# Three tile pairs instead of two, and keys' sums with the values stationary: one change to an attention and gated-MLP kernel on one Trainium2 core

## The chip, the cores and the metric

The kernel runs on one core of one Trainium2 chip. The core has a matrix engine (PE, in the code `nc.tensor`, TensorE) with its own queue for loading the stationary operand (PEld), a vector engine (DVE, `nc.vector`, VectorE), an activation engine (ACT, `nc.scalar`, ScalarE), a third elementwise engine (POOL, `nc.gpsimd`, GpSimd) and a queue that issues transfers (SP, `nc.sync`, SyncE). The metric is the device time of one execution in microseconds; lower is better. Each engine works through its own queue in order. The order in a queue is not quite that of the Python code: a planner (Tile) lists the instructions as they become ready, gives buffers out, and sets the semaphores.

## What is computed

Two things, one after the other: an attention with positive random features for 8 batches, 8 heads, 576 positions and 64 dimensions (128 features), and a gated MLP over its 4608 rows (512 to 1536 and back to 512). Cut to what matters:

```python
def phi(x):                                     # x is q or k, scaled
    h = einsum('bhsd,md->bhsm', x, omega) - sum(x * x, -1) / 2
    return exp(h - max(h, -1)) / sqrt(m)
q_p, k_p = phi(q), phi(k)
kv  = einsum('bhsm,bhsd->bhmd', k_p, v)         # keys' sums
z   = sum(k_p, axis=2)                          # (b, h, m)
num = einsum('bhsm,bhmd->bhsd', q_p, kv)
den = einsum('bhsm,bhm->bhs', q_p, z)[..., None] + 1e-06
x   = (num / den) as 4608 rows of 512
out = (silu(x @ w_gate) * (x @ w_val)) @ w_out
```

The three weights come as 64-bit floats.

## The kernel before

**Attention.** A head pair and 256 positions make a group (`kgroups`, `qgroups`, lines 115 to 117); each batch has nine groups of keys and nine of queries, the ninth (`None`) holding the left-over 64 positions of all four head pairs. `steps` (lines 124 to 127) puts two groups into each of 72 steps: keys alone in the first six, then a query and a key group, queries alone in the last six. A step n loads its rows (`load`, `load_v`), transposes them on PE (`st_transpose`, L400), copies them to x (ACT, L408), projects them (`st_project`, L423, two matmul instructions for each fp32 product), takes the maximum on DVE (`st_max`, L437 to L447) and the exponential on ACT (`st_exp`, L459, eight activations a step). `k_accumulate` (L561) takes the keys' features `ph` as the stationary operand and the values `vt`, 64 columns and a column of ones, as the moving one; so the 65th column of the sum is z. When a batch's half is whole, `kv_finalize` copies it out of PSUM.

**Two ways to divide.** For batches 0 to 3 (`b < BPOOL`) `q_mult` multiplies queries by kv and z at once and DVE divides. For batches 4 to 7 the queries' features are divided beforehand: `kv_finalize` transposes the z column (L481), ACT copies it (L483), SP writes it to DRAM (`zd`) and `load_z` reads it back to all 128 partitions (`zt`); `q_den` multiplies by it on POOL (L521, L517), reduces on DVE, and `q_norm` scales `ph` (L537). `q_out` (L642) then forms the output columns with kv stationary, 64 columns wide, one head in each half of PE's columns.

**MLP.** The 4608 rows are nine tiles of 512 columns. Each fp32 factor is split in a high and a low part (ACT casts, POOL or DVE subtracts), and each product is three matmul instructions of 512 columns. A *direct* tile is visited once for each of four sets of three of the twelve feature blocks (`stream`): 36 instructions for the gate, 36 for the value (`mm1`, L678), 36 for the way down (`mm2`, L687) of the previous visit. `ROUNDS` lists the direct tiles. `PAIRS` lists pairs of tiles for which gate and value go by seven half-size products (Strassen) instead of eight (`pair_rounds`, `product`, L912); the way down is as for direct tiles. Both have to load and split weights: before each new set, `load_weights` fetches a block from DRAM and at once emits the cast and the subtraction (`split_piece`, L251, L252).

**Pacing.** Attention and direct tiles are interleaved by hand. Up to step `EARLY` (25) a step holds attention only (`CLOSE`); afterwards each step goes through `GROUPED`, with six `SHARE` places at which `give` lets the MLP stream run on. How much is due is `course`: a taut line from step `EARLY` to the end of attention (step 76) through what is available, ending `MARGIN` = 45 us before the work of the direct tiles. `clock` and `marks` spread the conversion of the 36 weight blocks from 64 bits (`convert_all`, six ticks each: ACT L277 and L289, DVE L280 to L286, POOL L291) along the same line. When attention is over its buffers are given back, `first_x` prepares the first pair, and the pairs follow.

**Queues at the start.** `load_v` issues the first step's values, and the left-over values of a step below `AHEAD` (6), from ACT's queue; all other loads from SP's. In the first six steps there is one such left-over group, in step 2: four issues (L365). `setup_omega` (L337) and the copies of x follow in ACT's queue.

Of the kernel before, what the change touches and what calls it, by code (L numbers as in the profile page):

```python
# [11 lines left out]
F32 = mybir.dt.float32  # L12
# [4 lines left out]
ALU = mybir.AluOpType  # L17
# [6 lines left out]
def kernel(  # L24
# [37 lines left out]
    ROUNDS = [range(0, 3), range(3, 5)]  # L62
    PAIRS = [(5, 6), (7, 8)]
# [32 lines left out]
    make_identity(nc, ident)  # L96

# [211 lines left out]

    def load_weights(f, i):  # L310
        need(f, i)
        fetched = fetch((f,), i)
        new_weights(f, i)
        split_piece(f, i, fetched[0])
# [78 lines left out]
    def st_transpose(n):  # L393
# [11 lines left out]
        st = att.tile([P, 4, 2, CH, 2], F32, name=f"st_{n}", tag="st", bufs=6)  # L405
# [66 lines left out]
    def kv_finalize(b, a2):  # L472
        acc = kvacc.pop((b, a2))
        raw = att.tile([P, 4, VW], F32, name=f"kvr{b}_{a2}", tag="kvr", bufs=4)
        nc.scalar.copy(raw, acc)
        for j in range(2):
            kvst[b, 2 * a2 + j] = raw[:, 2 * j : 2 * j + 2, :]
        if b >= BPOOL:

            zp = ps_att(f"zp{b}_{a2}", [4, P])  # L480
            nc.tensor.transpose(zp, raw[:, :, D], ident)  # L481
# [6 lines left out]
    zds = {}  # L488
    zbc = {}

    def load_z(n):

        for _, b, g, gr in slots(n, "q"):
            if g == 0 and b >= BPOOL:
                zt = att.tile([P, 2, 4, M], F32, name=f"zt{b}", tag="zt")
                for a2 in range(2):
                    nc.sync.dma_start(
                        zt[:, a2], zds.pop((b, a2)).rearrange("(o h) m -> o h m", o=1).broadcast_to([P, 4, M])
                    )
                    zbc[b, a2] = zt[:, a2]  # L500
# [42 lines left out]
    def k_accumulate(n, half):  # L543

        n -= KLAG
        ks = [(b, g, gr, c) for _, b, g, gr in slots(n, "k") for c in range(CH)]
# [24 lines left out]
        return bool(slots(n, "k"))  # L571
# [133 lines left out]
    def down(j, k_, ht, wts, next_set, tt):  # L705
        fs = sorted(ht)
        po = ps_moe(f"o{j}_{k_}_{tt}", [P, DM])
        for n, f in enumerate(fs):
            need(f, 2)
            mm2(po, ht[f], weights[f, 2] if wts is None else wts[f], tt, n == 0, n == len(fs) - 1)  # L710
# [14 lines left out]
    def stream():  # L725

        todo = []
        for vi, (j, s_, k_) in enumerate(visits):
# [15 lines left out]
            for f in fs:  # L744
                need(f, 0)
                pg[f] = ps_moe(f"g{vi}_{f}", [P, T])[:, 0:w]
                mm1(pg[f], weights[f, 0], xs)
                yield mm1_us(w)
# [16 lines left out]
            for f in fs:  # L765
                need(f, 1)
                pv = ps_moe(f"v{vi}_{f}", [P, T])[:, 0:w]
# [11 lines left out]
            if final:  # L779
                make_seven((0, 0), 1, fetch((0, 1), 1))  # L780
            wts = {f: weights[f, 2] for f in fs} if vi else None
# [269 lines left out]
    def give(us):  # L1051
        debt[0] += us
        while debt[0] > 0:
            u = next(ma, None)
            if u is None:
                debt[0] = 0.0
                return False
            debt[0] -= u
# [50 lines left out]
    for n in range(NN):  # L1109
# [17 lines left out]
        load_z(n)  # L1127
# [41 lines left out]
```

## Time and profile before

| what | value |
|---|---|
| runs | 1180.82, 1174.82, 1174.39 us; median 1174.82 |
| the profiled execution: its time, its span | 1172.79 us, 1171.0 us |
| busy: PE, DVE, ACT, POOL | 98%, 54%, 58%, 49% of the span |
| first PE projection (start of step 0) | 8.83 us |
| steps 0 to 24, attention alone | 8.83 to 116.28 us |
| steps 25 to 71, with the direct tiles | from 116.28 us; step 71 begins at 703.48 us |
| pairs | from 797.31 us |

The table's stretches were read off the timeline: a step begins with the first of its 16 matmuls of L423, and the pairs with the first matmul of L912. In all views times are microseconds from the start of the span, "mean ns of one" is nanoseconds, and `x` in front of a number counts instructions. A matmul's busy time in the profile is longer than its share of the engine, because neighbours overlap; what a matmul costs is read from start to start.

### The profile page before, as it was taken

The page shows a single profiled execution, that of the slowest core. Times are in us where ns is not written, and L with a number is a line of the kernel's source. Part 1 is how long each engine was busy: PE and PEld are TensorE (multiplying, and loading weights), DVE is VectorE, ACT ScalarE, POOL GpSimd, SP SyncE. Part 2 cuts the span into 40 slices and gives each one's busy share as a digit, 9 for nine tenths or more (in the row PEclk, how much of TensorE's full clock was granted, in tenths as well). Part 3 has the DMA queues.
Part 4 walks back from the last instruction along what each step waited for, and adds up shares of the span by engine and source line. Part 5 has one row for each costly group of instructions (what it writes and reads, how often), then busy time and mean ns, then how long its engine had stood idle before and what let it go on. Part 6 is the DMA issues. An engine that isn't in the chain of part 4 may idle for free.

```text
span 1171.0 us, 18724 instructions
## 1 busy us (share of the span) xinstructions
PE 1149.5 (98%) x6705; PEld 951.7 (81%) x6705; DVE 630.0 (54%) x1159; ACT 678.3 (58%) x1499; POOL 569.1 (49%) x500
## 2 busy tenths in 40 slices
PE   7999999999999999999999999999999999999998
PEld 6998778888888888888888777878778888888886
DVE  5876667535466554334332552462566666456654
ACT  5898887775666665665466665334544445444441
POOL 3342353433365465554445765244655543455551
PEclk9999999999999999999999999999999999999999
DMA  7654355643454442443232212424311112211103
GB/s 168 155 147 116 108 168 164 177 127 111 127 155 131 125 118 70 120 105 82 64 80 73 60 46 81 127 81 123 93 53 47 48 53 54 72 55 54 45 19 73
DMA packets 174109, 113.52 MB, mean 97 GB/s; under 512 B 125856, under 2 KB 144320, under 8 KB 174016
## 3 DMA queue, kind: packets, MB, share of 16 engines
q1 hardware_dynamic: 172096, 111.86, 35.2%
q8 instruction: 53, 0.87, 0.3%
q10 hardware_dynamic: 1920, 0.46, 0.2%
q14 instruction: 40, 0.33, 0.1%
HBM read 87.10 MB, written 25.18 MB: 96 GB/s over the span
## 4 chain that ended last, share of the span: by engine, by line
PE 73%; DVE 5%; ACT 3%; DMA 2%; issue 2%; POOL 1%; SPq 1%; POOLq 0%; DVEq 0%; ACTq 0%
PE o L687 22%; PE g L678 11%; PE a L912 10%; PE v L678 10%; PE c L912 5%; PE pp L423 3%; PE d L912 3%; PE kvacc L561 2%; PE ptq L585 2%; PE xt L642 2%; PE pt L400 1%; DMA wraw<-wscr 1%; ACT ph L459 1%; DMA first_b<-xs 1%; POOL wlo L252 1%
## 5 line engine op out<-in xcount | busy, mean ns | idle before, releaser
L407 POOL TENSOR_TENSOR sq<-nat 128x512 f32<-128x512 f32 x72 | 75.9, 1055 | 199.3 <-DVE st L437 157.3
L716 DVE TENSOR_TENSOR acc<-o,acc 128x512 f32<-128x512 f32 x140 | 95.6, 687 | 128.6 <-PE o L687 128.2
L459 ACT ACTIVATE ph<-pp,st 128x128 f32<-128x128 f32 x576 | 157.0, 387 | 6.4 <-DVE st L447 5.7
L444 DVE TENSOR_REDUCE st<-pp 128x4 f32<-128x512 f32 x144 | 93.3, 686 | 95.7 <-PE pp L423 95.4
L252 POOL TENSOR_TENSOR wlo<-wraw,whi 128x512 fp32r<-128x512 f32 x76 | 103.1, 1366 | 64.0 <-ACT whi L251 62.4
L678 PE MATMUL g<-xh,whi 128*128 128x512 f32 x240 | 96.3, 401 | 0.9 <-DVE sl L771 0.9
L678 PE MATMUL v<-xh,whi 128*128 128x512 f32 x240 | 95.6, 398 | 0.5 <-DVE acc L716 0.5
L687 PE MATMUL o<-whi,hh 128*128 128x512 f32 x240 | 95.9, 400 | 0.0
L423 PE MATMUL pp<-omT,x 64*128 64x128 f32 x1152 | 90.9, 289 | 4.6 <-ACT x L408 4.6
L687 PE MATMUL o<-whi,hl 128*128 128x512 f32 x240 | 93.8, 391 | 0.9 <-POOL hl L775 0.9
L775 POOL TENSOR_TENSOR hl<-sl,hh 128x512 fp32r<-128x512 f32 x60 | 77.9, 1302 | 33.7 <-ACT hh L774 33.5
L678 PE MATMUL g<-xl,whi 128*128 128x512 f32 x240 | 94.0, 392 | 0.0
L678 PE MATMUL g<-xh,wlo 128*128 128x512 f32 x240 | 94.0, 392 | 0.0
L678 PE MATMUL v<-xh,wlo 128*128 128x512 f32 x240 | 93.9, 391 | 0.0
L687 PE MATMUL o<-wlo,hh 128*128 128x512 f32 x240 | 93.9, 391 | 0.0
L678 PE MATMUL v<-xl,whi 128*128 128x512 f32 x240 | 93.6, 390 | 0.0
L423 PEld LDWEIGHTS pp<-omT,x 64*128 64x128 f32 x1152 | 73.9, 189 | 21.8 <-issue 11.6
L899 POOL TENSOR_TENSOR wlo<-wspare,whi 128x512 fp32r<-128x512 f32 (+1 forms) x40 | 40.5, 1032 | 75.0 <-ACT whi L898 68.6
L771 DVE TENSOR_TENSOR sl<-v,sl 128x512 f32<-128x512 f32 x60 | 40.9, 685 | 60.8 <-PE v L678 60.8
L251 ACT CAST whi<-wraw 128x512 fp32r<-128x512 f32 x76 | 46.6, 629 | 42.1 <-PE v L678 24.4
L525 DVE TENSOR_REDUCE dj<-jk 128x4 f32<-128x512 f32 x36 | 24.6, 685 | 83.8 <-POOL jk L521 69.1
L774 ACT CAST hh<-sl 128x512 fp32r<-128x512 f32 x60 | 37.5, 626 | 51.9 <-DVE sl L771 51.7
(257 smaller groups left out, 2938.4 us busy)
## 6 DMA issues: line engine op xcount, KB each, us to landing
wraw<-wscr SPq DMA_DIRECT2D x80, 256.0 KB, 2.7
wspare<-wscr SPq DMA_DIRECT2D x40, 256.0 KB, 2.7
wscr<-wc SPq DMA_DIRECT2D x36, 256.0 KB, 2.2
out_dram<-acc SPq DMA_DIRECT2D x72, 128.0 KB, 2.3
nat<-in_k_dram SPq DMA_DIRECT2D x64, 128.0 KB, 3.1
nat<-in_q_dram SPq DMA_DIRECT2D x64, 128.0 KB, 3.1
v<-in_v_dram SPq DMA_DIRECT2D x62, 128.0 KB, 3.0
st<-in_moe_w_gate_dram SPq DMA_DIRECT2D x12, 512.0 KB, 3.9
```

Source lines behind the costliest of these rows:

```text
L251: nc.scalar.copy(hi, raw)
L252: nc.gpsimd.tensor_tensor(lo, raw, hi.bitcast(F32), op=ALU.subtract)
L407: nc.gpsimd.tensor_tensor(sq, nat, nat, op=ALU.mult)
L423: nc.tensor.matmul(pp[hh][:, i, c, :], x[r, i, c * P : (c + 1) * P], omT[r], start=True, stop=True)
L444: nc.vector.tensor_reduce(st[:, 1, :, :, hh], pp[hh], axis=AX.X, op=ALU.max, negate=True)
L459: step_end["s"] = nc.scalar.activation(ph[:, c, hh * M : (hh + 1) * M], pp[hh][:, i, c, :], AF.Exp, bias=st[:, 3, i, c, hh : hh + 1], scal ...
L678: nc.tensor.matmul(ps, a_[:, ws], b_[:, c, :], start=n == 0, stop=n == 3 * NC - 1)
L687: nc.tensor.matmul(ps, a_[:, ts_], b_, start=first and n == 0, stop=last and n == 2)
L716: nc.vector.tensor_tensor(a_, po, a_, op=ALU.add)
L771: nc.vector.tensor_tensor(h, pv, h, op=ALU.mult)
L775: nc.gpsimd.tensor_tensor(hl, h, hh.bitcast(F32), op=ALU.subtract)
L912: nc.tensor.matmul(ps, a_[:, w_], b_[:, c, :], start=start and c == 0 and m == 0, stop=c == CH - 1 and m == 2, skip_group_check=True,)
```

## The change

It has five parts.

1. **Rounds and pairs.** Tiles 3 and 4 leave the direct rounds and become a third pair, the first one.
2. **Keys' sums, batches 4 to 7.** `k_columns` takes the values as the stationary operand (64 columns; the two heads of a pair in the two halves of PE's columns) and the features as the moving one (128 columns). The sum is then transposed; `kv_turn` copies it out to `x`-tagged SBUF and transposes it back with four PE transposes a batch.
3. **z, batches 4 to 7.** `z_sum` adds up the features on DVE into two tiles a batch; `z_spread` multiplies each by a matrix of ones (fp32, 512 columns), which sums over the partitions and spreads the result over all of them; ACT copies it to `zt`. The transposes, the DRAM round trip and `load_z` are gone.
4. **Weights.** `load_weights` only issues the fetch; `land`, called at each unit of the stream, emits cast and subtraction three units later, or earlier when the weights are needed.
5. **Left-over values** by SP, also in the first steps; and `st` has three buffers instead of six.

```diff
-    ROUNDS = [range(0, 3), range(3, 5)]
-    PAIRS = [(5, 6), (7, 8)]
+    ROUNDS = [range(0, 3)]
+    PAIRS = [(3, 4), (5, 6), (7, 8)]
...
+    ones = const.tile([P, P], F32, name="ones")
+    nc.vector.memset(ones, 1.0)
...
     def load_weights(f, i):
         need(f, i)
-        fetched = fetch((f,), i)
-        new_weights(f, i)
-        split_piece(f, i, fetched[0])
+        landing.append([LAND, f, i, fetch((f,), i)[0]])
+
+    def land(upto=None):
+
+        for t in landing:
+            t[0] -= upto is None
+        while landing and (landing[0][0] <= 0 or upto in [(f, i) for _, f, i, _ in landing]):
+            _, f, i, raw = landing.pop(0)
+            new_weights(f, i)
+            with behind_step():
+                split_piece(f, i, raw)
...
-            load_group(t, v, b, gr, True, nc.scalar if n == 0 or n < AHEAD and gr is None else nc.sync)
+            load_group(t, v, b, gr, True, nc.scalar if n == 0 else nc.sync)
...
-        st = att.tile([P, 4, 2, CH, 2], F32, name=f"st_{n}", tag="st", bufs=6)
+        st = att.tile([P, 4, 2, CH, 2], F32, name=f"st_{n}", tag="st", bufs=3)
...
-        if b >= BPOOL:
-
-            zp = ps_att(f"zp{b}_{a2}", [4, P])
-            nc.tensor.transpose(zp, raw[:, :, D], ident)
-            zs = att.tile([4, P], F32, name=f"zs{b}_{a2}", tag="zs")
-            nc.scalar.copy(zs, zp)
-            zd = dram.tile([4, P], F32, name=f"zd{b}_{a2}", tag="zd", bufs=4)
-            nc.sync.dma_start(zd, zs)
-            zds[b, a2] = zd
...
+    def z_sum(n):
+
+        for _, b, g, gr in slots(n - 1, "k"):
+            if b < BPOOL:
+                continue
+            ph = box["k", b, g]
...
+            with behind_step():
...
+                pr, r = gr
+                to = zsums[b, pr // 2][:, pr % 2]
+                if pr < 2 and r == 0:
+                    nc.vector.tensor_tensor(to, ph[:, 0], ph[:, 1], op=ALU.add)
+                else:
+                    for c in range(CH):
+                        nc.vector.tensor_tensor(to, ph[:, c], to, op=ALU.add)
+
+    def z_spread(n):
+
+        for b, a2 in list(zsums):
+            if n != (qstep[b, 2] + JLAG if a2 else qstep[b, 0]):
+                continue
+            zp = ps_att(f"zp{b}_{a2}", [P, 4, M])
+            nc.tensor.matmul(
+                zp.rearrange("p h m -> p (h m)"), ones, zsums.pop((b, a2)).rearrange("p j m -> p (j m)"),
+                start=True, stop=True,
+            )
+            zbc[b, a2] = att.tile([P, 4, M], F32, name=f"zt{b}_{a2}", tag="zt", bufs=3)
+            nc.scalar.copy(zbc[b, a2], zp)
+
+    def k_columns(n):
+
+        for _, b, g, gr in slots(n - KLAG, "k"):
...
+            for c in range(CH):
+                for j, pr in enumerate(pairs_of(gr)[c]):
+                    for hh in range(2):
+                        nc.tensor.matmul(
+                            acc[hh * D : (hh + 1) * D, pr, :],
+                            vt[:, 2 * c + j if gr is None else c, hh, 0:D],
+                            ph[:, c, hh * M : (hh + 1) * M],
...
+            if done[b] == 2 * NACC:
+                turned[b] = att.tile([P, NPAIR, M], F32, name=f"kvt{b}", tag="x")
+                nc.scalar.copy(turned[b], kvacc.pop(b))
+
+    def kv_turn(n):
+
+        b, o = divmod(n - (AHEAD - 1), NG)
+        if o or b not in turned:
+            return
+        kt = turned.pop(b)
+        pt = ps_att(f"kvp{b}", [P, 2, 4, D])
+        for pr in range(NPAIR):
+            nc.tensor.transpose(
+                pt[:, pr // 2, 2 * (pr % 2) : 2 * (pr % 2) + 2].rearrange("p h d -> p (h d)"), kt[:, pr], ident
+            )
+        for a2 in range(2):
+            raw = att.tile([P, 4, VW], F32, name=f"kvr{b}_{a2}", tag="kvr", bufs=4)
+            nc.scalar.copy(raw[:, :, 0:D], pt[:, a2])
...
     GROUPED = (
         q_out,
+        k_columns,
         st_project,
         q_transpose,
         lambda n: k_accumulate(n, 0),
         lambda n: k_accumulate(n, 1),
+        kv_turn,
+        z_spread,
         st_max,
+        z_sum,
         st_exp,
         q_den,
...
-        load_z(n)
```

`land((f, i))` also stands behind each `need(f, i)` in `stream` and `down`, and once for the blocks of the way down ahead of each later visit; `give` calls `land()` for each unit. `k_accumulate` skips batches 4 to 7.

More of the change, by code (lines that the diff above doesn't have):

```diff
@@ new lines @@
+    zsums = {}
+    qstep = {(b, g): n for n in range(NS) for _, b, g, _ in slots(n, "q")}
+    turned = {}
+    def z_sum(n):
[3 more added lines that the diff above has]
+            ph = box["k", b, g]
+            if gr is None or gr == (0, 0):
+                a2 = 0 if gr else 1
+                zsums[b, a2] = att.tile([P, 2, 2 * M], F32, name=f"zs{b}_{a2}", tag="zs")
+                if a2:
+                    nc.gpsimd.memset(zsums[b, a2], 0.0)
+            with behind_step():
+                if gr is None:
+                    for c in range(CH):
+                        for j in range(2):
+                            rows = slice(j * RES, (j + 1) * RES)
+                            to = zsums[b, c][rows, j]
+                            nc.vector.tensor_tensor(to, ph[rows, c], to, op=ALU.add)
+                    continue
[6 more added lines that the diff above has]
+                        nc.vector.tensor_tensor(to, ph[:, c], to, op=ALU.add)
@@ new lines, in k_columns @@
+    def k_columns(n):
+        for _, b, g, gr in slots(n - KLAG, "k"):
+            if b < BPOOL:
+                continue
+            ph, vt = box.pop(("k", b, g)), vrows[b, g]
+            busy.remove(vt)
+            if b not in kvacc:
+                kvacc[b] = ps_k.tile([P, NPAIR, M], F32, name=f"kvt{b}", tag="kv")
+                done[b] = 0
+            acc = kvacc[b]
+            for c in range(CH):
+                for j, pr in enumerate(pairs_of(gr)[c]):
[4 more added lines that the diff above has]
+                            ph[:, c, hh * M : (hh + 1) * M],
+                            start=done[b] == 0,
+                            stop=LAST[pr] == (g, c),
+                            skip_group_check=True,
+                        )
+                    done[b] += 1
+            if done[b] == 2 * NACC:
+                turned[b] = att.tile([P, NPAIR, M], F32, name=f"kvt{b}", tag="x")
+                nc.scalar.copy(turned[b], kvacc.pop(b))
@@ new lines, in kv_turn @@
+    def kv_turn(n):
[7 more added lines that the diff above has]
+                pt[:, pr // 2, 2 * (pr % 2) : 2 * (pr % 2) + 2].rearrange("p h d -> p (h d)"), kt[:, pr], ident
+            )
+        for a2 in range(2):
+            raw = att.tile([P, 4, VW], F32, name=f"kvr{b}_{a2}", tag="kvr", bufs=4)
+            nc.scalar.copy(raw[:, :, 0:D], pt[:, a2])
+            for j in range(2):
+                kvst[b, 2 * a2 + j] = raw[:, 2 * j : 2 * j + 2, :]
@@ L545, in k_accumulate @@
         n -= KLAG
-        ks = [(b, g, gr, c) for _, b, g, gr in slots(n, "k") for c in range(CH)]
+        ks = [(b, g, gr, c) for _, b, g, gr in slots(n, "k") for c in range(CH) if b < BPOOL]
         for b, g, gr, c in ks[half * len(ks) // 2 : (half + 1) * len(ks) // 2]:
@@ L570, in k_accumulate @@
                     kv_finalize(b, a2)
-        return bool(slots(n, "k"))
+        return bool(ks)
     qts = {}
@@ L745, in stream @@
                 need(f, 0)
+                land((f, 0))
                 pg[f] = ps_moe(f"g{vi}_{f}", [P, T])[:, 0:w]
@@ L766, in stream @@
                 need(f, 1)
+                land((f, 1))
                 pv = ps_moe(f"v{vi}_{f}", [P, T])[:, 0:w]
@@ L780, in stream @@
                 make_seven((0, 0), 1, fetch((0, 1), 1))
+            for f in fs if vi else ():
+                land((f, 2))
             wts = {f: weights[f, 2] for f in fs} if vi else None
@@ L1057, in give @@
                 return False
+            land()
             debt[0] -= u
```

14 lines of the change are left out of this document (4 added, 10 removed).

## The prediction

> **What bounds the kernel now.** First the page: the span, busy times, then the chain that ended last.
>
> ```profile
> span 1171.0 us, 18724 instructions
> PE 1149.5 (98%) x6705; PEld 951.7 (81%) x6705; DVE 630.0 (54%) x1159; ACT 678.3 (58%) x1499; POOL 569.1 (49%) x500
> ...
> PE 73%; DVE 5%; ACT 3%; DMA 2%; issue 2%; POOL 1%; SPq 1%; POOLq 0%; DVEq 0%; ACTq 0%
> ```
>
> PE sets the time, but a busy share of 98% says little, since a matmul's busy time overlaps its neighbour's. So I look next at what one matmul costs from start to start, in the chain by order of time during the pairs:
>
> ```profile
> 870.08 1.36 PE o L687 x6
> ```
>
> Six 512-column instructions take 1.36 us: 0.2267 us each. That price turns any stretch into MLP work and the rest. The windows by stage, then the same windows for L678 and L687 alone (length; PE, PEld, DVE, ACT, POOL busy with counts; granted clock; DMA share; GB/s):
>
> ```profile
> 116.28:208.41 92.13, 88.59 (x606) 73.63 (x605) 62.41 (x131) 74.24 (x170) 37.95 (x33) 1.00 0.51 144
> 200.18:208.41 8.23, 8.23 (x61) 7.12 (x60) 4.72 (x12) 6.43 (x18) 2.08 (x2) 1.00 0.45 120
> 208.41:348.01 139.60, 138.31 (x864) 116.16 (x863) 70.64 (x141) 91.49 (x200) 61.31 (x52) 1.00 0.51 143
> 426.84:637.91 211.07, 210.85 (x1287) 171.85 (x1285) 78.94 (x165) 123.27 (x275) 108.87 (x96) 1.00 0.34 86
> 875.00:1150.00 275.00, 275.00 (x1215) 227.72 (x1214) 161.56 (x225) 123.41 (x221) 141.97 (x117) 1.00 0.17 49
> ```
> ```profile
> 116.28:208.41 92.13, 36.27 (x138) 24.46 (x137) 1.00 0.51 144
> ...
> 208.41:348.01 139.60, 75.24 (x312) 57.45 (x312) 1.00 0.51 143
> ```
> ```profile
> 116.28:208.41 92.13, 18.62 (x72) 13.00 (x72) 1.00 0.51 144
> 200.18:208.41 8.23, 4.65 (x18) 3.23 (x18) 1.00 0.45 120
> 208.41:348.01 139.60, 26.05 (x108) 19.91 (x108) 1.00 0.51 143
> ```
>
> One step without a stall (200.18, 18 MLP matmuls) takes 8.23 - 18 x 0.2267 = 4.15 us beside its filler. Nine steps from 116.28 hold 210 MLP matmuls: 92.13 - 47.6 - 9 x 4.15 = 7.2 us of stalls, 0.80 a step; there ACT is busy 74.24 of the 84.9 us that the work needed, 87%. Ten steps from 208.41 hold 420: 139.60 - 95.2 - 41.5 = 2.9 us, 0.29 a step, at ACT 67%. In the sixteen steps from 426.84 PE idles 0.2 us, ACT at 58%. In the pairs PE never idles; DVE is busy 59%, the rest less. So the kernel pays for PE's instructions, plus about 10 us of stalls where steps are short and ACT is crowded.
>
> **Part 1, the third pair.** A direct tile takes 12 x 12 instructions for the gate, as many for the value and for the way down, 432; two take 864. A pair takes 7 products x 6 instructions x 2 x 6 blocks = 504, and 288 for the way down: 792. The 72 that go are worth 72 x 0.2267 = **-16.3 us**, all on PE's path. The pair's additions lie on DVE, ACT and POOL, which the last pairs' row shows covered; if that cover were gone, DVE at 59% would have to grow by two thirds first. The change of pair lies within 875 to 1150 already once, at no cost, and now comes twice.
>
> What it moves is the filler. Attention keeps its 51 later steps, but only twelve visits of 108 instructions lie between them: (293.8 - 45) / 51 = 4.88 us a step, where it was 5.4 in the first nine and 9.4 afterwards ((489.7 - 45 - 48.9) / 42). Steps shorten from about 13 to about 8.4 us, and what the other engines do for attention is packed closer. The question is what ACT then has to do in a step. ACT's groups in the sixteen steps, by form, and the two conversion groups of the page:
>
> ```profile
> L459 ACT ACT_TABLE_LOAD x10 | 12.8, 1283 | 0.2
> L752 ACT ACT_TABLE_LOAD x9 | 11.5, 1283 | 1.3 <-PE g L678 1.1
> L774 ACT CAST hh<-sl 128x512 fp32r<-128x512 f32 x18 | 11.2, 622 | 20.0 <-DVE sl L771 19.9
> L752 ACT ACTIVATE sl<-g 128x512 f32<-128x512 f32 x18 | 10.6, 597 | 9.5 <-PE g L678 8.6 <-POOL ph L537 0.8
> ...
> L251 ACT CAST whi<-wraw 128x512 fp32r<-128x512 f32 x15 | 9.3, 627 | 11.6 <-PE v L678 6.0 <-PE o L687 2.8 <-DMA wraw<-wscr 1.5
> L702 ACT CAST xh<-xraw 128x512 fp32r<-128x512 f32 x8 | 4.8, 618 | 1.7 <-PE v L678 1.3 <-DMA xraw<-xs 0.3
> L713 ACT COPY acc<-o 128x512 f32<-128x512 f32 x8 | 4.7, 608 | 3.3 <-PE o L687 3.2
> ```
> ```profile
> L289 ACT ACTIVATE st<-st 128x512 int32<-128x512 uint32 x36 | 26.0, 722 | 0.0
> L277 ACT ACTIVATE wc<-st 128x512 f32<-128x512 f32 x36 | 25.6, 712 | 7.2 <-POOL wlo L252 7.2
> ```
>
> Without these seven groups ACT's 123.27 us leave 58.4, or 3.65 a step for attention. A fifth of a visit adds 0.2 x (3 x 0.597 + 3 x 0.622) = 0.73, its table loads (24.3 us in six visits) 0.8, 27 casts of weights over 51 steps 0.33, 0.6 conversion pieces of 1.43 us 0.86 (the marks spread them to step 66), the new copies 0.15: 6.5 of 8.4 us, 78%. The nearest rows are 67% (0.29 a step) and 87% (0.80). But both lie in batches 0 to 3, where DVE's division stands between PE's product and the next transposition; later q_out takes what ACT copied a step before. I take 0.65 for steps 25 to 35, 0.4 for the nine to 44, 0.25 for the 21 to 65, nothing after: 16 us, against 10 now, **+6 us**. Ends: -10 (no stalls at all) and +31 (51 x 0.80 - 10.1).
>
> [...] The trace:
>
> ```profile
> 412.32 0.62 ACT L774 CAST hh<-sl 128x512 fp32r<-128x512 f32 x1 [2.55 <-DVE sl L771]
> 413.04 1.28 ACT L752 ACT_TABLE_LOAD   x1
> 414.33 0.60 ACT L752 ACTIVATE sl<-g 128x512 f32<-128x512 f32 x1
> ```
>
> [...]
>
> **Part 2, keys' sums.** Timeline of one step, PE and ACT's copy of ptq (start, length, operands, count):
>
> ```profile
> 401.15 0.65 PE L642 MATMUL xt<-qt,kvr 128*64 128x256 f32 x4
> 401.73 1.16 PE L423 MATMUL pp<-omT,x 64*128 64x128 f32 x16
> 402.82 0.66 PE L585 MATMUL ptq<-ident,ph 128*128 128x128 f32 x4
> 403.31 1.00 PE L561 MATMUL kvacc<-v,ph 128*128 128x65 f32 x8
> 403.51 0.58 ACT L587 COPY qt<-ptq 128x512 f32<-128x512 f32 x1 [0.78 <-PE ptq L585]
> 404.15 0.61 PE L400 MATMUL pt<-ident,nat 128*128 128x128 f32 x4
> ```
> ```profile
> L481 PE MATMUL zp<-ident,kvr 128*4 128x128 f32 x8 | 2.2, 272 | 0.4 <-ACT kvr L475 0.2
> ```
>
> A group's eight instructions take 404.15 - 403.31 = 0.84 us from start to start; a batch has eight such groups and one of double size, so batches 4 to 7 pay 40 x 0.84 = 33.6 us. The new form isn't in the trace. Nearest is pp: 128 columns moving as well, two halves of the array side by side (rows there): 16 in 1.09 us, so 8 in 0.55. xt uses column halves: 4 x 256 columns in 0.58 us, the same 1024 columns. I take 0.55: 40 x 0.55 = 22, **-11.6 us**. Ends: 0.42 (half of now, -16.8) and 1.09, halves one after the other (+10). [...]
>
> z: the eight transposes go, -2.2. Eight multiplications by ones, two instructions of 512 columns each, come. xt's four instructions fill three places in a row (same head twice, then the other), 0.19 us for 256 columns, so 0.77 for one z; pp the same way, nine places of 128 columns, 0.97. I take 0.85: **+6.8** (4.6 to 9.3: xt's columns at full overlap, and without any). kv_turn: 16 transposes, by ptq (403.31 - 402.82 = 0.49 for four) +2.0. These products use the PSUM buffer that ptq has just filled; ACT's copy of it ends 403.51 + 0.58 - 403.31 = 0.78 us after ptq, beside kvacc's 0.84, which now stands earlier. Twelve places wait for up to 0.8 (0 to +9.6); pt and filler can go ahead, as the older transposes' row shows (0.4 us of waits in eight), so +2. Sum of the part: -11.6 - 2.2 + 6.8 + 2.0 + 2 = **-3.0 us**.
>
> DVE's sums, two a step:
>
> ```profile
> L612 DVE TENSOR_TENSOR xn<-po,dn 128x256 f32<-128x256 f32 x36 | 15.2, 422 | 1.0
> ```
>
> add 0.84 us to DVE's 78.94/16 = 4.9, which loses about as much filler work and gains 0.9 of conversion: some 70% of 8.4, behind the step's bias, so nothing on PE's path while DVE stays under ACT. SP loses zd and zt: nothing waited for them.
>
> **Part 3, weights cast later.** ACT no longer stands at a cast whose transfer is under way (1.5 us of 11.6 above). PE uses the weights visits later: 0, with up to -2 in the stalls counted.
>
> **Part 4, the start.** Order of time, ACT's queue and what waits:
>
> ```profile
> 3.30 3.40 ACTq L365 DMA_DIRECT2D vrest<-in_v_dram  x4
> ...
> 8.20 0.58 ACT L408 COPY x<-pt 128x512 f32<-128x512 f32 x1
> 8.66 3.41 SPq L358 DMA_DIRECT2D v<-in_v_dram  x5
> 8.83 2.08 PE L423 MATMUL pp<-omT,x 64*128 64x128 f32 x16 [3.55 <-ACT x L408]
> ```
>
> Four issues hold ACT for 3.40 us, then the table, omT and x follow, and PE's first projection. Without them it could begin up to 2.9 us earlier (x needs the transposes too, and the table still has to come). But SP takes the four issues over ahead of later q and k loads, and is itself issuing without a break; its delay (3.4) would show some steps later. **-1.5 us** (-2.9 to +0.5).
>
> **Sum.** 1171.0 - 16.3 + 6 - 3.0 - 1.5 = 1156.2 us of span, and the 1.8 us by which the profiled execution's 1172.79 exceeds its span: **1158.0 us**. The profiled execution is 2.0 us under the median 1174.82, 1.6 under the fastest run; half a percent, 6 us, is about what a measurement tells from no change.
>
> **The rivals.**
> *Starved steps (slower).* All 51 steps stall as the nine from 116.28 do, because ACT and DVE cannot do a step's exponentials, splits and conversions in 8.4 us: 0.80 x 51 - 10.1 = 31 in place of 6: 1183.0 us. It decides at (20.8 + 10.1) / 51 = 0.61 a step, where the 20.8 us of the other terms are eaten up. For it: ACT at 78% by my count. Against: the step at 200.18 is as short and has no stall. 0.14. [...]
> *Halves in turn.* The column halves do not run side by side, so the swap doesn't do what it is written for: +10 instead of -11.6, 1179.6 us. Against: xt's 0.58. 0.03.
> *No stalls.* Casts behind their loads and even filler clear the stalls: -10 for +6, start -2.9: 1140.6 us; half of that 1149. For it: the row at 200.18. 0.15.
> *The forecast*, 1149 to 1169: 0.68.
>
> The range takes in the first half of the stall-free case and of the starved one: 1146 to 1173. Faster by over 0.5% (below 1169): 0.80; within: 0.09; slower: 0.11.
>
> **What would show it.** L912 should count 1512 instead of 1008, L678 864 instead of 1440. The pairs should last 3 x 792 x 0.2267 = 539 us; k_columns 0.55 us a group; the first pp should come near 6 to 7 us; steps 45 to 65 should last near 8.5 us with few PE waits. Wrong if PE waits for ACT's x, ph or qt in most steps, if ACT passes 90% there, or if the first pair starves at its start.

## The result, and the profile after

The changed kernel takes 1185.72 us (median of 7 runs, 1176.89 to 1191.43); the kernel before, run beside it on the same chip, 1174.79 us (7 runs, 1173.34 to 1180.82). The ratio is 1.0074 with the interval [1.0053, 1.0096]: slower by 0.7%, where 1158.0 us was forecast. The profiled execution, 1191.43 us, is the slowest of its seven; its start alone, up to step 25, is 8.5 us longer than before, which no other kernel of this study repeats: for 17.1 us from 34.7 on its clock stands at half. So the trace says where time is lost, and the ratios say how much.

The page of the changed kernel, the lines that answer to those shown of before, with PE's clock in 40 slices and one group each of gate and products:

```profile
span 1189.6 us, 18961 instructions
PE 1147.2 (96%) x6657; PEld 942.0 (79%) x6657; DVE 739.9 (62%) x1339; ACT 689.7 (58%) x1545; POOL 591.5 (50%) x519
...
PEclk9799999999998999899999999999999999999999
...
PE 75%; DVE 11%; ACT 4%; POOL 3%; issue 3%; DMA 2%; SPq 1%; POOLq 0%; DVEq 0%; ACTq 0%
...
L757 PE MATMUL g<-xh,whi 128*128 128x512 f32 x144 | 60.9, 423 | 0.0
```
```profile
L996 PE MATMUL a<-t3hi,whi 128*128 128x512 f32 x72 | 28.2, 392 | 0.4 <-ACT late L1092 0.4
```

Six such gate and value groups of 144 make 864 instructions, and 21 groups of 72 make 1512 in the products: both counts are as forecast. PE has less to do (busy 1147.2 where it was 1149.5, though some of it ran at a lower clock, 0.984 of full speed on average), and the span is 18.6 us longer. The chain that ended last has DVE with 11% of the span (5% before) and POOL with 3% (1%): PE waits for them now. The 8s of PEclk are the other trace of this; before, the granted clock was 1.00 up to 1169.6 us of the span's 1171.0. The 7 is the start (length; PE, PEld, DVE, ACT, POOL busy with counts; granted clock; DMA share; GB/s):

```profile
34.70:51.70 17.00, 17.00 (x99) 16.09 (x96) 7.56 (x20) 9.01 (x26) 5.21 (x5) 0.50 0.62 158
```

Steps 7 to 9 take 19.9 us there and 12.3 before, 7.6 of the 8.5 us.

The prediction's own measure splits the span: the length of a stretch, less 0.2267 us for each 512-column MLP instruction in it, is what attention's instructions and all stalls cost there. Read off the traces (all in us; "idle" is PE's idle time in steps 25 to 70, and the last column the half-clock stretches that begin between step 25 and the pairs):

| kernel | to step 25 | steps 25 to 70 | idle | 71 to attention's end | half clock |
|---|---|---|---|---|---|
| before | 116.3 | 191.0 | 5.1 | 7.6 | none |
| after | 124.8 | 212.4 | 22.8 | 11.3 | 164.4, 372.6 (6.8 us), 492.1 (6.8 us), 574.0 |
| rounds and pairs only | 120.4 | 201.4 | 11.6 | 11.6 | 159.5, 391.6, 558.9 |
| all but the new sums | 118.4 | 201.3 | 11.5 | 9.7 | 520.9 |
| sums and z later | 118.7 | 201.3 | 16.1 | 9.7 | 381.3 |
| before, waits put in the pairs | 119.0 | 190.8 | 5.2 | 7.6 | none |

A stretch is 3.4 us long where nothing else is said. So the 16.3 us of matmuls are gone, and 21.4 come back in steps 25 to 70, 3.7 behind them and 8.5 ahead of them (in this execution). The waits of PE between step 25 and 71 (us in total, times, longest), after:

```profile
PE zp L530 <- ACT qt L666: 6.3, 4, 3.6
PE ptq L664 <- POOL ph L616: 5.3, 3, 3.4
PE pt L413 <- ACT xo L736: 3.8, 3, 1.9
PE ptq L664 <- ACT xo L736: 2.8, 3, 2.1
PE pt L413 <- issue: 2.4, 1, 2.4
...
PE kvp L572 <- ACT qt L666: 1.1, 2, 0.9
```

and before, the same view:

```profile
PE pt L400 <- DVE xl L664: 1.2, 1, 1.2
PE xt L635 <- DVE xn L612: 1.1, 1, 1.1
```

The first and the last row of after belong to the new z and the turned-back sums, the second to queries' features that POOL scales; the kernel before has none of the three.

**The longest wait.** Order of time, the changed kernel, PE and ACT with what releases them:

```profile
366.78 0.61 PE L551 MATMUL kvt<-ph,v 128*64 128x128 f32 x8
...
367.32 1.16 PE L436 MATMUL pp<-omT,x 64*128 64x128 f32 x16
...
368.41 0.66 PE L664 MATMUL ptq<-ident,ph 128*128 128x128 f32 x4
...
369.80 0.40 PE L766 MATMUL o<-whi,hl 128*128 128x512 f32 x1
...
372.62 0.62 ACT L253 CAST whi<-wraw 128x512 fp32r<-128x512 f32 x1 [5.25 <-DMA wraw<-wscr]
...
373.14 0.58 ACT L666 COPY qt<-ptq 128x512 f32<-128x512 f32 x1
...
373.77 2.07 PE L530 MATMUL zp<-zs,ones 128*128 128x512 f32 x2 [3.57 <-ACT qt L666]
```

k_columns' eight instructions take 367.32 - 366.78 = 0.54 us, as forecast (0.55). ptq is done at 369; its copy qt stands in ACT's queue right behind a cast of weights that itself waited 5.25 us for a transfer. So zp, which wants ptq's PSUM buffer, waits 3.57 us, and with it, in PE's queue, the filler behind it. The forecast had taken 0.78 us from ptq to the end of its copy, and 2 us of waits for all twelve places.

**What follows the wait.** The windows around it, in the same columns as above:

```profile
366.50:372.60 6.10, 3.70 (x39) 2.79 (x35) 5.01 (x9) 0.40 (x2) 5.17 (x5) 1.00 0.40 115
372.60:379.40 6.80, 5.63 (x11) 3.81 (x12) 3.44 (x6) 4.82 (x13) 3.84 (x3) 0.50 0.66 171
379.40:386.00 6.60, 6.60 (x52) 5.21 (x51) 4.61 (x13) 2.38 (x6) 2.64 (x2) 1.00 0.14 40
```

For 6.8 us the granted clock is 0.50. The 512-column instructions start 0.43 us apart in it (376.07, 376.50, 376.93) and 0.23 us apart behind it (379.47, 379.70, 379.94). So the wait is paid for a second time.

**The second longest wait** has the other cause. DVE and POOL in order of time:

```profile
485.67 2.69 DVE L514 TENSOR_TENSOR zs<-ph,zs 64x256 f32<-64x256 f32 x2
486.62 2.88 POOL L600 TENSOR_TENSOR jk<-ph,zt 128x512 f32<-128x512 f32 x2
488.39 1.38 DVE L522 TENSOR_TENSOR zs<-ph,zs 128x256 f32<-128x256 f32 x1
489.70 0.67 DVE L604 TENSOR_REDUCE dj<-jk 128x4 f32<-128x512 f32 x1
490.29 0.66 DVE L522 TENSOR_TENSOR zs<-ph,zs 128x256 f32<-128x256 f32 x1
490.95 0.67 DVE L604 TENSOR_REDUCE dj<-jk 128x4 f32<-128x512 f32 x1
...
491.85 2.04 POOL L616 TENSOR_TENSOR ph<-ph,dj 128x512 f32<-128x512 f32 x2 [1.18 <-DVE dj L605]
...
492.94 1.11 PE L664 MATMUL ptq<-ident,ph 128*128 128x128 f32 x4 [3.41 <-POOL ph L616]
```

Three of z's additions take 4.07 us ahead of the first reduction and a fourth stands between the two; the divisors come late, POOL scales ph late, and PE waits 3.41 us for it. Each of the three takes 1.3 to 1.4 us beside POOL's work; alone one takes 0.42 (below).

### The profile page after: what moved, and what is told of

Same layout as the page of the kernel before. It is cut to its first block, busy times and chain, and to the rows that moved or that the text cites. A ratio compares the mean times of both kernels' runs of the same rounds, so it can differ in the third digit from the quotient of the medians.

```text
span 1189.6 us, 18961 instructions
## 1 busy us (share of the span) xinstructions
PE 1147.2 (96%) x6657; PEld 942.0 (79%) x6657; DVE 739.9 (62%) x1339; ACT 689.7 (58%) x1545; POOL 591.5 (50%) x519
## 4 chain that ended last, share of the span: by engine, by line
PE 75%; DVE 11%; ACT 4%; POOL 3%; issue 3%; DMA 2%; SPq 1%; POOLq 0%; DVEq 0%; ACTq 0%
PE o L766 21%; PE a L996 15%; PE c L996 8%; PE v L757 5%; PE pp L436 5%; PE g L757 4%; PE d L996 4%; PE po L681 2%; PE ptq L664 2%; PE kvacc L640 2%; PE pt L413 2%; ACT ph L472 2%; DVE st L457 1%; DMA nat<-in_k_dram 1%; PE xt L721 1%
## 5 line engine op out<-in xcount | busy, mean ns | idle before, releaser
L983 POOL TENSOR_TENSOR wlo<-s,whi 128x512 fp32r<-128x512 f32 x64 | 82.4, 1308 | 3.8 <-ACT whi L982 3.8
L1092 ACT COPY late<-a 128x512 f32<-128x512 f32 x72 | 42.2, 586 | 60.3 <-PE a L996 59.1
L766 PE MATMUL o<-whi,late 128*128 128x512 f32 x192 | 74.5, 389 | 0.0
L666 ACT COPY qt<-ptq 128x512 f32<-128x512 f32 x72 | 41.6, 587 | 38.8 <-PE ptq L664 38.4
L766 PE MATMUL o<-whi,hh 128*128 128x512 f32 x144 | 59.7, 415 | 1.0 <-ACT sl L833 0.8
L757 PE MATMUL v<-xh,whi 128*128 128x512 f32 x144 | 58.7, 408 | 0.0
L293 POOL TENSOR_TENSOR wc<-st 128x512 int32<-128x512 int32 x36 | 37.8, 1050 | 41.0 <-ACT st L291 23.3
L757 PE MATMUL v<-xl,whi 128*128 128x512 f32 x144 | 57.9, 402 | 0.0
L757 PE MATMUL g<-xh,wlo 128*128 128x512 f32 x144 | 57.8, 401 | 0.0
L413 PE MATMUL pt<-ident,nat 128*128 128x128 f32 x288 | 47.9, 289 | 10.0 <-ACT xo L736 3.8
```

The lines of the kernel that those rows point to most:

```text
L413: nc.tensor.transpose(pt[:, i, c * P : (c + 1) * P], nat[:, i, c].rearrange("p h d -> p (h d)"), ident)
L757: nc.tensor.matmul(ps, a_[:, ws], b_[:, c, :], start=n == 0, stop=n == 3 * NC - 1)
L766: nc.tensor.matmul(ps, a_[:, ts_], b_, start=first and n == 0, stop=last and n == 2)
L983: nc.gpsimd.tensor_tensor(lo, src_, hi.bitcast(F32), op=ALU.subtract)
```

## The experiments

Three theories. **A**: the new sums stall PE, by the shared PSUM buffer (A1) or by DVE's additions (A2). **B**: the short steps do it by themselves. **C**: part of the loss is the clock, which falls behind waits; where an expectation speaks of C at the start, it means a fall of the clock there that it puts down to the start's new transfers. Medians and ratios are against runs of the kernel before on the same chip; its medians were 1174.1 to 1176.2 us.

### Rounds and pairs only

```diff
 (the kernel before)
-    ROUNDS = [range(0, 3), range(3, 5)]
-    PAIRS = [(5, 6), (7, 8)]
+    ROUNDS = [range(0, 3)]
+    PAIRS = [(3, 4), (5, 6), (7, 8)]
```

> The kernel before with only the rounds and pairs changed: three direct tiles, three pairs. Theory A (the new z and key sums stall PE: the shared PSUM buffer, DVE's sums): these are not in it, so the 16.3 us of the 72 matmuls show nearly whole, 1160 to 1164 us. Theory B (steps with half the filler starve by themselves, whatever the keys' sums do): 1172 to 1185 us, PE waits spread over steps 34 to 70. Theory C (the start's new transfers make PE idle and its clock fall): the start is the older one, step 25 begins near 116 us at clock 1.00, time as under A.

Measured: 1174.81 us, ratio 0.9986 [0.9965, 1.0008]. By the ratio that is 1.6 us under the kernel before (-4.1 to +0.9): of the 16.3 us nearly all are given back by this part alone, as B expects. Windows over steps 44 to 65, before and here:

```profile
348.01:637.91 289.90, 289.64 (x1758) 235.51 (x1757) 124.75 (x251) 174.44 (x385) 150.63 (x132) 1.00 0.36 95
```
```profile
302.02:499.21 197.19, 192.47 (x1318) 155.24 (x1317) 122.11 (x247) 141.51 (x342) 123.24 (x109) 0.99 0.46 127
```

These 22 steps hold 912 MLP instructions before and 471 here: 3.78 and 4.11 us a step beside them, +7.3 us in all. ACT's 141.51 us are 6.43 a step, the 6.5 of the forecast; the loss of 0.33 a step is near the 0.25 that it took. But steps 66 to 70, where it took nothing, cost 4.58 instead of 3.73 us each (+4.3), and the time from step 71 to attention's end grows from 7.6 to 11.6 (+4.1); steps 25 to 43 change by -1.1. Of the 10.4 us in steps 25 to 70, 6.5 are idle time of PE, and two stretches at half clock (3.4 us each) can make some 3.3. In the last steps the MLP's split stands in ACT's queue ahead of attention's copies:

```profile
554.89 0.60 PE L585 MATMUL ptq<-ident,ph 128*128 128x128 f32 x4
555.25 0.47 PE L678 MATMUL v<-xl,whi 128*128 128x512 f32 x1
558.21 0.66 PE L585 MATMUL ptq<-ident,ph 128*128 128x128 f32 x4 [2.49 <-ACT xo L657]
```
```profile
557.26 0.62 ACT L774 CAST hh<-sl 128x512 fp32r<-128x512 f32 x1 [2.55 <-DVE sl L771]
557.79 0.36 ACT L657 COPY xo<-xt 128x256 f32<-128x256 f32 x1
```

The copy xo waits behind a cast that waits 2.55 us for DVE; the second ptq wants xo's buffer. Behind this wait the clock is at half for 3.4 us. The steps of 13 us before the change show no such wait.

### Shorter steps still

```diff
 (rounds and pairs only)
-    MARGIN = 45.0
+    MARGIN = 95.0
```

> The kernel before with the new rounds and pairs alone (1174.81 us), and MARGIN 95 instead of 45: the direct tiles then leave 95 us for the time after attention, so each of the 51 short steps gets 0.98 us less of MLP work ((293.8 - 95) / 51 = 3.90 us, where it was 4.88). Nothing is added or taken away. Theory B, density: the stalls come from ACT and DVE having too little time in a short step, so they grow again when the step shrinks from about 8.4 to 7.4 us: from 0.25 a step to the 0.80 a step of the crowded stretch before the change, at least 15 us, 1188 to 1200 us. Rival: they sit at a few places (a cast behind its transfer, one step with an unexplained 2.4 us, the tail of attention) that do not depend on the length of the steps: within 3 us of 1174.81, and PE's waits between step 25 and 71 near the 11.6 us seen.

Measured: 1188.54 us (4 runs), ratio 1.0124 [1.0107, 1.0142], at the lower end of what B expects and far from the rival. The same instructions, with 0.98 us less filler in a step, cost 13.7 us more by the medians and 16 by the ratios. In the traces, steps 25 to 70 give 8.7 of it (210.1 for 201.4), but PE's idle time only 2.0 (13.6 for 11.6), and the half-clock time in them is the same, 6.8 us; the stretch of MLP work between attention and pairs gives 3.8. So the density of the steps has a price by itself. Most of it lies where PE shows as busy, in instructions that follow one another more slowly: pp's alone take 3.8 us more from start to start. What holds them back was not followed further.

### All but the new sums

```diff
 (the kernel after; keys' sums, z and its round trip as before the change)
-        k_columns,
...
-        kv_turn,
-        z_spread,
...
-        z_sum,
...
+        load_z(n)
```

> The changed kernel with the older key sums and z (features stationary, z through DRAM); third pair, late casts and left-over v as changed. Theory A: the waits for zp, kvp and the late scaled ph are gone, 1163 to 1168 us apart from the start. Theory B: still starved, 1178 to 1188 us. Theory C: as A plus 8 us when the clock falls at the start.

Measured: 1174.57 us, ratio 1.000 [0.9976, 1.0024], between A and B. Against the kernel after (1.0074) the new sums cost about 0.7%, 9 us by the ratios and 11 by the medians, where the forecast gave them -3.0. In steps 25 to 70 they cost 212.4 - 201.3 = 11.1 us, and PE's idle time grows by 11.3: in the short steps the sums lose by waiting and by the clock behind the waits (17.1 us at half clock in these steps of after, 3.4 here), not by their instructions.

### The new sums in long steps

```diff
 (the kernel after)
-    ROUNDS = [range(0, 3)]
-    PAIRS = [(3, 4), (5, 6), (7, 8)]
+    ROUNDS = [range(0, 3), range(3, 5)]
+    PAIRS = [(5, 6), (7, 8)]
```

> The changed kernel with the older rounds and pairs: five direct tiles, two pairs; key sums, z, late casts and left-over v as changed. Theory A: the z products wait in long steps too, slower than before by 5 to 10 us, 1180 to 1185. Theory B: with 13 us steps nothing starves, and the cheaper key sums show: 1170 to 1174. Theory C: slower than before by about 8 us through the start alone, clock below 1.00 between 25 and 75 us.

Measured: 1178.34 us, ratio 1.0014 [0.9998, 1.003]: in steps of 13 us the same sums, with late casts and SyncE's values, cost 1.6 us (-0.2 to 3.5); that lies between the two expectations. The short steps without the sums end at 1.000 and the sums in long steps at 1.0014; together they are at 1.0074, some 7 us more than the two added up. (Late casts and SyncE's values are in all three; no run has them alone.)

### Left-over values on ACT's queue again

```diff
 (the kernel after)
-            load_group(t, v, b, gr, True, nc.scalar if n == 0 else nc.sync)
+            load_group(t, v, b, gr, True, nc.scalar if n == 0 or n < AHEAD and gr is None else nc.sync)
```

> The changed kernel with the left-over v of the first steps issued by ACT again. Theory C: the clock stays at 1.00 from 25 to 75 us, step 25 begins near 116 us instead of 124.8, and the median falls by 6 to 8 us to about 1178. Theories A and B: the later waits and clock falls stay, the median stays within 3 us of 1185.

Measured: 1183.91 us (5 runs), ratio 1.0082 [1.0053, 1.011], not to be told from after, as A and B have it. The start holds no half-clock stretch here, but that isn't the edit's doing: of the eight other kernels with SyncE's values only one has such a stretch before step 25, of 3.4 us, and two of the five without them have 6.8 us. The 17.1 us in after belong to its one profiled execution. In the traces the first projection begins at 6.2 to 7.3 us in all kernels that have this part, and at 8.8 to 9.3 without it; but by step 5 the gain is gone (27.19 in "all but the new sums", 25.65 before).

### Weights cast at once

```diff
 (the kernel after)
-        landing.append([LAND, f, i, fetch((f,), i)[0]])
+        fetched = fetch((f,), i)
+        new_weights(f, i)
+        split_piece(f, i, fetched[0])
```

> The changed kernel with weights cast right at their fetch, as before. If the late casts matter (ACT standing at a cast whose transfer is under way delays ptq's copy and so zp), the waits of ACT for wraw grow from 7.9 us and the median rises to 1188 or more. If they don't, the median stays within 3 us of 1185.

Measured: 1180.16 us, ratio 1.0041 [1.0023, 1.0059]: 0.3% less than after, the intervals overlapping slightly, and outside both expectations. The later casts did not help. ACT stands less at casts whose transfers are under way (7.9 us, 2 times, after; 13.9 us, 7 times, here), but zp's waits for qt are as long (6.3 and 6.0 us).

### No sums for z

```diff
 (the kernel after, in z_sum: of all additions only the first of a tile is left)
-                else:
-                    for c in range(CH):
-                        nc.vector.tensor_tensor(to, ph[:, c], to, op=ALU.add)
```

> The changed kernel with nearly all of DVE's z sums left out (one addition for each of the first groups stays, so z is wrong). Theory A2 (the sums make DVE late with the divisors, so that PE waits for POOL's scaled ph, 5.3 us, with a fall of the clock behind it): those waits go, median 1175 to 1179. Rival (DVE has room, as forecast): within 3 us of 1185.

Measured: 1174.88 us, ratio 0.9993 [0.9978, 1.0008], with the sums for z left out. Compared with after, 0.8% go, as A2 expects. PE's waits of ptq for POOL's ph fall from 5.3 to 2.1 us, but zp's for qt stay at 5.5:

```profile
PE zp L522 <- ACT qt L658: 5.5, 4, 3.7
...
PE ptq L656 <- POOL ph L608: 2.1, 1, 2.1
```

### The spreading of z and the turned-back sums later

```diff
 (the kernel after)
-            if n != (qstep[b, 2] + JLAG if a2 else qstep[b, 0]):
+            if n != qstep[b, 2 if a2 else 0]:
...
-        kv_turn,
-        z_spread,
         st_max,
...
         lambda n: st_transpose(n + 1),
         SHARE,
         SHARE,
+        kv_turn,
+        z_spread,
         SHARE,
```

> The changed kernel with kv_turn and z_spread behind the second SHARE of a step, when ACT has long copied ptq out of the shared PSUM buffer. Theory A1 (they wait in PE's queue for that copy): the waits zp for qt (6.3 us) and kvp for qt (1.1) go, and the clock's fall behind the longest (6.8 us at half): 1174 to 1178 us. Rival (the copy is late because all engines are crowded, and the next product then waits as long): the waits move to ptq, pt or pp, 1182 us or more.

Measured: 1173.51 us (10 runs), ratio 0.9985 [0.9967, 1.0002], 0.9% under after with the same instructions. Its waits, the same view as above:

```profile
PE pt L413 <- ACT xo L736: 4.9, 4, 1.8
PE ptq L664 <- ACT xo L736: 2.6, 2, 2.1
...
PE zp L530 <- ACT qt L666: 1.3, 1, 1.3
```

The first line of the edit moves more than the text of the expectation says: the second spreading of each batch, four of eight, comes two shares later in the step before, so earlier by most of a step. The one with the longest wait (3.57 us) is a first spreading, moved by the two shares alone.

zp's wait falls from 6.3 to 1.3 us, kvp's only from 1.1 to 0.9, and the one for POOL's ph is not among the rows any more, though DVE's additions are all there. They take 36.0 us in all where they took 43.5, and three of them over 1.2 us where it was 14; whether the earlier second spreadings did this, by giving POOL its zt sooner, was not tried by itself. So the place of eight products and sixteen transposes decided most of the loss. A1 and A2 are not separate sums: this edit brings 0.9%, leaving z's additions out 0.8%, and the new sums cost 0.7% in all. Each wait moves the others, and the clock with them (one half-clock stretch is left here, four in after).

### The same, with weights cast at once

The two edits above together.

> The kernel after with two parts altered: the turned-back sums and the spreading of z stand two shares of MLP work later in the step (as in the run before that took 1173.51 us), and the weights are cast right behind their fetch, as before the change (alone 1180.16 us). Theory A1 and the late casts as separate costs: the two gains, 12.2 and 5.5 us against 1185.72, add up to 17.7, so 1168 us, below the kernel before (1176). Rival: both gains come from the same waits (PE behind ACT's qt copy, where ACT stood at a late cast), so the second adds nothing: 1172 to 1175 us. By the first, PE's waits for ACT between step 25 and 71 fall below the 11 us that the kernel with late z still has, to about 6, and no stretch at half clock is left; by the rival the gap stays at 10 to 16 us.

Measured: 1175.5 us (12 runs), ratio 0.9986 [0.9969, 1.0004]: the gains do not add up, as the rival has it, and three half-clock stretches are left where the first theory wants none. zp even waits 4.5 us for qt, 3.1 at 361.7 us, where ACT had stood 4.29 us at a cast for its transfer. So the late casts' 0.3% may have been scatter or a chance of places; that is open.

### The later place, in long steps

The edit of "later" with the old rounds and pairs.

> Two pairs and five direct tiles as before the change, with the new sums of keys, z on DVE, late casts and left-over values by SyncE, and the turned-back sums and the spreading of z two shares later in the step. With the places as in the change this mix took 1178.34 us (1.4 per mille over the kernel before). Theory A1: what the new sums lose in long steps is the wait behind ACT's qt copy; moved, the part is worth its instructions (-11.6 - 2.2 + 9.3 + 2.0, near -2.5 us) and the mix takes 1172 to 1175 us. Rival: the loss is z's spreading and DVE's additions themselves, whatever their place: 1177 to 1179 us.

Measured: 1176.55 us (12 runs), ratio 0.9992 [0.9976, 1.0009]. This lies between the two expectations, and its interval overlaps that of the old place (1.0014): not settled. (The 9.3 us for z in the expectation is too much by the trace, see below.)

### z's additions later as well

```diff
 (the kernel with z later)
         st_max,
-        z_sum,
         st_exp,
...
         q_mult,
         SHARE,
+        z_sum,
         SHARE,
```

> The kernel with the turned-back sums and z's spreading two shares later (1173.51 us), and DVE's additions for z moved as well, from between the maximum and the exponential to behind the division and the first share that follows it. The same instructions in all. Theory A2 (DVE's additions, 0.42 us each alone and 1.2 to 1.4 us when POOL works beside them, hold up the reductions that the divisors and POOL's scaled features wait for): the additions fall where less waits for them, PE's idle time between step 25 and 71 goes from 16.1 us to about 11 to 13, and the time to 1169 to 1172 us. Rival: with z's spreading moved nothing that PE needs waits for the additions any more (that kernel shows no wait of ptq for POOL's ph), so within 1.5 us of 1173.5.

Measured: 1171.97 us (12 runs, 1171.05 to 1180.04), ratio 0.997 [0.9951, 0.9988]: of all versions the only one whose interval lies below the kernel before, by 0.3%. That the additions' place did it is not shown: PE's idle time in steps 25 to 70 is 17.9 us, where A2 wants 11 to 13 and it was 16.1; these steps are as long as without this edit (201.8 for 201.3 us), the two profiled spans are the same, 1170.2 us, and the intervals of the two versions overlap. In its profiled execution no half-clock stretch comes before the end.

### Waits put into the pairs

```diff
 (the kernel before; pair_rounds, behind the last product of eight half-visits)
+                        if i == 1 and vi in WAITS:
+                            nc.scalar.copy(chain, a[:, 0:P])
+                            for _ in range(WAITS[vi]):
+                                nc.scalar.copy(chain, chain)
+                            pw = ps_w.tile([P, T], F32, name=f"pw{vi}", tag="w")
+                            nc.tensor.transpose(pw[:, 0:P], chain, ident)
```

with 4, 8, 12 and 16 copies at two places each.

> The kernel before, with eight waits put into PE's queue during the pairs: PE needs the end of a chain of 5, 9, 13 or 17 small ACT copies of its last product, each length twice; nothing else changes. Theory C (a wait costs more than itself, as the clock falls to half behind it): half-clock stretches of 3.4 us or more follow the longer waits and none the 5-copy ones, and those waits cost 1.7 us or more above their own length. Rival (a wait costs just its length; the clock falls for another reason): clock 1.00 throughout the pairs.

Measured: 1194.23 us (2 runs), ratio 1.0157 [1.0122, 1.0191]. The chain's length didn't set the wait: PE stood seven times, for 1.51 to 1.84 us, once for the chain and six times for the accumulation on DVE (acc) that frees a buffer of the way down. Four of these waits, all of 1.83 or 1.84, were followed by a stretch at half clock; those of 1.51 and 1.69, and the last of 1.84, were not. One of the four, PE in order of time, and the clock in windows around it:

```profile
922.15 0.39 PE L687 MATMUL o<-whi,hl1k 128*128 128x512 f32 x1
924.36 0.50 PE L687 MATMUL o<-whi,hh0k 128*128 128x512 f32 x1 [1.83 <-DVE acc L716]
...
927.01 0.63 PE L912 MATMUL a<-b11hi,wlo 128*128 128x512 f32 x1
927.44 0.63 PE L912 MATMUL a<-b11hi,whi 128*128 128x512 f32 x1
...
928.70 0.39 PE L912 MATMUL c<-t1lo,whi 128*128 128x512 f32 x1
928.92 0.39 PE L912 MATMUL c<-t1hi,wlo 128*128 128x512 f32 x1
```
```profile
921.60:924.90 3.30, 1.47 (x7) 0.93 (x6) 3.27 (x5) 3.11 (x10) 3.01 (x3) 0.97 0.25 79
924.90:928.30 3.40, 3.40 (x10) 2.58 (x10) 0.60 (x2) 0.34 (x2) 0.00 (x0) 0.52 0.21 77
928.30:931.70 3.40, 3.40 (x17) 2.81 (x16) 0.00 (x0) 3.04 (x7) 1.85 (x2) 1.00 0.02 5
```

Behind the wait matmuls start 0.43 us apart, and 0.22 us apart 3.4 us later. About eight at 0.43 instead of 0.227 make some 1.6 to 1.7 us: C holds, and by this estimate such a wait of 1.83 us cost some 3.5. The pairs last 391.8 us where they lasted 369.4; of the 22.4 us, 12.5 are idle time, and the four stretches make some 6.6 of the rest.

Which waits bring the clock down, the traces of all kernels together show. In each trace the half-clock stretches begin whole multiples of 3.413 us apart: in after at 164.40, 372.61, 492.08 and 574.00, so 208.21, 119.47 and 81.92 us apart, which is 61, 35 and 24 times 3.413, the length of the stretches at 164.40 and 574.00 themselves. Taken as a grid, this cuts a trace into intervals. In the fourteen traces, from step 25 to 10 us before the end, 29 half-clock stretches begin. Each begins at the end of an interval in which PE idled for 1.55 us or more (in after 1.77, 2.41, 2.55 and 2.13 us). All 21 intervals with 1.87 us or more of idle time were followed by one, eight of the 15 between 1.55 and 1.85, and none of some 4200 with less. So what counted in these traces is how much of a wait fell into one interval. In the trace of this run, an interval that holds a whole wait of 1.83 us, and the two between which the last wait, of 1.84, is divided:

```profile
921.32:924.73 3.41, 1.58 (x8) 1.00 (x7) 3.38 (x5) 3.08 (x10) 3.18 (x3) 1.00 0.24 77
1146.60:1150.01 3.41, 3.26 (x15) 2.37 (x13) 3.38 (x5) 1.74 (x5) 3.17 (x3) 1.00 0.01 2
1150.01:1153.42 3.41, 1.72 (x7) 1.42 (x8) 2.85 (x5) 3.09 (x12) 2.16 (x2) 1.00 0.00 0
```

PE idles 1.83 us in the first (3.41 - 1.58), 0.15 and 1.69 us in the others; the clock falls behind the first alone. In the same way one wait of 2.4 us (pt, put down to "issue") stands in nine of the traces, and the clock falls behind it in three.

## Why the prediction was wrong

From before to after the forecast saw -14.8 us of span; by the ratio the change brings +8.7. The runs build it up one part at a time: rounds and pairs alone 0.9986, with late casts and SyncE's values 1.000, with the new sums 1.0074. Of the miss of some 24 us, the sums have about 12 and the rounds about 9; late casts and the start the rest, each known to 2 or 3 us by the ratios' intervals.

- **Third pair, -16.3.** Right. 1512 and 864 instructions; the pairs' 2412 matmuls, with a few left from the direct tiles, run from 634.4 to the end at 1189.6, 555.2 us, of which 8.5 are more than 0.2267 each, where it was 6.7 before (counted from 797.15, where the first matmul of L912 stands in the trace). The pairs aren't starved at their start.
- **Crowded steps, +6 (-10 to +31).** Mis-sized, and at one place wrong. In the run with the rounds alone it is 10.4 in steps 25 to 70 and 4.1 behind them, 14.5. The load of ACT (6.5 us a step, 6.43 measured) and the 0.25 a step for the middle (0.33) were near, though the steps lasted 8.96 us and not 8.4; "nothing after" step 65 failed. There the steps are as short, and the same queue holds xo and qt behind a cast that waits for DVE. An engine's busy share was taken as the measure of stalls; ACT was busy 72% in steps 44 to 65, but what counted was which instruction it stood at. The rival of starved steps, 31, was too large for this kernel, though with one more microsecond off each step (MARGIN 95) it is nearly reached: 14.5 and some 14 to 16 more.
- **The new sums' instructions, -11.6 - 2.2 + 6.8 + 2.0.** Right within a microsecond: 0.54 to 0.59 us a group (0.55), the eight products for z 0.97 each at full clock by the matmuls around them (0.85), so 7.8 in all, and the turned-back sums 0.35 to 0.49 for four transposes.
- **Their wait for the PSUM buffer, +2 (0 to +9.6).** With the next one the step that failed most: the new sums were to bring -3.0 us, and they cost some 9. 7.4 us of idle time in after (6.3 for zp, 1.1 for kvp), inside the bounds but near the far end. The upper end was worked out from an ACT that copies ptq at once, 0.78 us later. It had not been asked what stands ahead of that copy in ACT's queue in a short step. A cast waiting 5.25 us for its transfer does. The edit that moved them shows that this was the place's price, not the products'.
- **DVE's additions, "nothing on PE's path".** Wrong. They are 72, 43.5 us in all, where 72 at 0.42 make 30.2: the 43 with no work of POOL beside them take 0.42, and 14 take 1.23 to 1.42. More than that, DVE's share (70% in steps 44 to 65 by its 144.12 us, as forecast) hid that the reductions for the divisors stand in the same queue, and POOL's scaling and ptq behind them: 5.3 us of waits that the kernel before doesn't have.

```profile
306.96:512.57 205.61, 191.86 (x1331) 150.38 (x1329) 144.12 (x293) 143.22 (x346) 125.75 (x112) 0.97 0.42 115
```

- **Late casts, 0 (up to -2).** No gain in either pair of runs; 0.3% against them in after, none with z later.
- **The start, -1.5 (-2.9 to +0.5).** The first projection did come 1.5 us earlier (7.32 us), and the delay did show some steps later; the net is not to be seen in the scatter of the starts, 116 to 125 us at step 25.
- **The clock.** The forecast had no term for it. In after, the stretches at half clock that begin between step 25 and the pairs are 3.4, 6.8, 6.8 and 3.4 us long, six units of 3.4. At the 1.6 to 1.7 us each that were estimated in the pairs they add up to some 10 us to waits of 2.38, 3.57, 3.41 and 2.13. Over the seven runs of after, time goes roughly with the granted clock: 1191.43 us at 0.984, 1176.89 at 0.998, the others from 0.989 to 0.994.

In steps 25 to 70 the pieces of the sums nearly close, against "all but the new sums": 11.3 us more idle time, up to 6.6 for four more units at half clock, and -4.0 of instructions make 13.9, where the trace of after has 11.1 more.

The rival of the slower side was named at its place (ACT in short steps), with too little time in all as its mechanism. The run with still shorter steps shows that this has a price too; but at 8.96 us a step ACT was busy 72%, and the long waits that were followed up come from the order in three queues, ACT's, DVE's and POOL's.

## What to carry to other kernels

A forecast for an added wait needs the whole queue of the engine that ends it, with that queue's own waits; the releasing instruction's duration is only the lower end (0.78 us to the end of ptq's copy in before, and a wait of 3.57 for it in after). When work is taken out between two dependent steps, count which waits it had covered, in every stage up to the last one, and price a new wait of PE at up to twice its length where it can put as much idle time into one interval as stood before the half-clock stretches here (1.55 us or more in 3.413; a wait of 1.83 us cost some 3.5 by the estimate in the pairs). A product that reuses a PSUM buffer belongs where its release has long happened: moving eight of them, with the turned-back sums, was worth 0.9%.

## What the runs showed of the hardware

From step 25 on PE's clock fell to half for 3.4 us, or twice that, in the middle of long busy stretches, behind intervals of a 3.413 us grid with 1.55 us or more of idle time: behind all 21 with at least 1.87 us, and 8 of the 15 below that. A wait of 2.4 us that was divided between two intervals cost no clock in six traces of nine. DVE's additions for z (128 or 64 x 256, 72 in after) took 0.42 us each where no instruction of POOL ran beside them, 43 in all; of the other 29, 14 took 1.23 to 1.42 us, two 0.66, and 13 no more than 0.42.
